# Channel attention and a gated convolution: v turned by VectorE instead of TensorE

## The chip, the cores and the metric

The kernel runs on one core of a Trainium2 chip. The metric is the device time in microseconds. Three runs of the kernel before took 652.89, 653.17 and 653.32 us; the median is 653.17 us.

Names used below: PE is TensorE, DVE is VectorE, ACT is ScalarE, POOL is GpSimd, and SP is SyncE, which here only issues transfers. A "step" is one chunk of the output's rows going through the second half of the kernel; a "group" is three rows per partition of q and k going through the first half.

## The reference

q, k and v have the shape 4 × 6336 × 256 (batch, row, channel), in float32.

```python
qn = q / (np.linalg.norm(q, axis=1, keepdims=True) + 1e-06)
kn = k / (np.linalg.norm(k, axis=1, keepdims=True) + 1e-06)
s = kn.transpose(0, 2, 1) @ qn / tau          # 256 x 256 for each batch
s = s - s.max(-1, keepdims=True)
a = np.exp(s)
a /= a.sum(-1, keepdims=True) + 1e-09
x = v @ a                                     # 6336 x 256 for each batch
gate_pre[t] = sum over 5 taps k of conv_w[k] * x[t - 4 + k]
gate = 1 / (1 + exp(-gate_pre))
out = (gate * (x @ w_val)) @ w_out
```

The attention is over channels: for each batch a matrix of 256 × 256 is made from all 6336 rows of q and k, and then all rows of v go through it.

## The kernel before

**Scores.** For each batch, partition p takes 49 rows of q and k, and 64 rows are left over. They go in 17 groups of up to three rows per partition (`score_group`). For a row, PE multiplies the 128 × 256 block of k (as weights, in two halves of 128 channels) with the block of q, and sums into a PSUM tile. A row is done in one of two ways. A native row multiplies the float32 data as they are (`nw` is the number of such rows in a group). A split row is first cut by ACT into a rounded high half in float32r (line 196) and by POOL into the remainder (line 197), and three products high·high, high·low and low·high follow. ACT squares q and k (line 213), and DVE and POOL add the squares up for the norms (line 218; `nv` rows of a group go to DVE). All of batch 0 is native but for the last row of its last two groups, and so are the first four groups of batch 1.

**Softmax.** `softmax` turns the sum into the attention matrix and a second matrix, attention times w_val, each as high and low halves. It is cut into stages that `tick` places between other work.

**Chunks.** The 6336 rows go in 13 chunks of up to 508 rows, 52 steps for the four batches. A chunk of v has four more rows ahead of it (the taps reach back). `load_v` brings it into SBUF with rows on partitions, in pieces of 1 KB. `transpose_v` turns it so that channels lie on partitions: PE transposes up to eight blocks of 128 × 128 into two PSUM tiles (line 359), ACT casts each into the high half (line 360), and DVE subtracts for the low half (line 361). `conv` multiplies with the attention matrix (six matmuls for each half of the output channels, line 369), and applies the taps: ACT the first (line 383), DVE the other four (line 385). `sigmoid` follows on ACT. `value` multiplies the same v with the second matrix (line 369 again) and DVE multiplies by the gate (line 398). `split_g` cuts the product into halves on ACT (line 411) and POOL (line 412). `finish` multiplies with w_out (line 428), ACT copies the result out of PSUM (line 438) and issues the stores.

**Order.** First come the 17 groups of batch 0; near their end the first chunks of v are loaded. Then the first four groups of batch 1 and the softmax of batch 0 are woven together. Then a loop over the 52 steps does for step n: load the chunk of v three steps on; one score group; the sigmoid of this step, the convolution of the next, the value and the split of this step; perhaps a second score group; the transposes of the chunk two steps on (`VLEAD` is 2); and `finish` of the step before. The score groups of all batches are spread over the first 36 steps, 47 groups in all, so the last steps have chunks alone. A planner, with its own model of times, places the instructions into each engine's queue; `behind` tells it to place work after a marked instruction, and `high_priority` raises a stage. Each engine works through its queue in order.

**Buffers.** The raw rows of q and k have six buffers, v's raw chunk three, the turned chunk three, the gate two. Four PSUM tiles are shared by the transposes, the values and the outputs; the convolution has two of its own. All loads are issued by SP in order, four groups ahead of use for q and k (`PREFETCH`).

Of the kernel before, what the change touches and what calls it, by code (L numbers as in the profile page):

```python
# [18 lines left out]
P = 128  # L19
# [3 lines left out]
VLEAD = 2  # L23
SIDE, LAST = 5, 15
# [5 lines left out]
def kernel(  # L30
# [76 lines left out]
    def load_weights(*names):  # L107
        for part in names:
            w = parts_w[part]
            if WORDS == 2:  # L110
                tag = {"val": "gate", "out": "o_sb"}.get(part)
                raw = (w_p if tag else const).tile([P, w.shape[1], WORDS], I32, name="w_raw", tag=tag or "c_raw")
            else:
                raw = w.rearrange("p (n o) -> p n o", o=1)
            w_raw[part] = raw
            if part == "conv":
                src = conv_w.bitcast(I32) if WORDS == 2 else conv_w
                nc.sync.dma_start(out=tau_sb, in_=tau.broadcast_to([P, 1]))
                for h in range(NH):
                    nc.sync.dma_start(out=raw[:, h * K:(h + 1) * K, :],  # L120
                                      in_=src[:, h * P * WORDS:(h + 1) * P * WORDS].rearrange("k (p o) -> p k o", o=WORDS))
            else:
                src = {"val": w_val, "out": w_out}[part]
                src = src.bitcast(I32) if WORDS == 2 else src
                nc.sync.dma_start(out=raw.rearrange("p (h e) o -> p h (e o)", h=NH),
                                  in_=src.rearrange("(h p) e -> p h e", p=P))
# [40 lines left out]

    state = {}

    def score_group(b, g):  # L170
# [4 lines left out]
        if b == 0:  # L175
            nw, nv = (2, 3) if g >= LAST else (GROUP, 2 if g < SIDE or g % 3 == 0 else 1)
        else:
            nw, nv = (GROUP, 1 if g else 2) if b == 1 and g < LEAD else (0, 2)
# [43 lines left out]
        def mms(np_, j):  # L222
            r = slice(0, np_)
            stop = g == NG - 1 and np_ == parts[-1][0] and j == parts[-1][1] + parts[-1][2] - 1
            for h in range(NH):
                hs = slice(h * P, (h + 1) * P)
                if j < nw:
                    ops = [(raw[r, j, 1, hs], raw[r, j, 0, :])]
                else:
                    ops = [(hi[r, j, 1, x, hs], hi[r, j, 0, y, :]) for x, y in ((0, 0), (0, 1), (1, 0))]  # L230
                for n_, (lhs, rhs) in enumerate(ops):
                    marks["PE"] = nc.tensor.matmul(st["s"][:, h, :], lhs, rhs, start=False,  # L232
                                                   stop=stop and h == NH - 1 and n_ == len(ops) - 1)
# [17 lines left out]
    def softmax(b):  # L251
# [9 lines left out]
        for x in range(2):  # L261
            for h in range(NH):
                marks["PE"] = nc.tensor.matmul(n_ps[:, x * NH + h:x * NH + h + 1], acc[:, x, h * P:(h + 1) * P], ones[:, 0:1],
                                               start=True, stop=True)
# [67 lines left out]
    vraw, vt = {}, {}  # L332

    def load_v(b, i):

        t0, w = chunks[i]
        t = raw_p.tile([P, NT, C], F32, name="v_raw", bufs=3)
        j0 = 0
        if i == 0:
            nc.gpsimd.memset(t[0:HALO, 0, :], 0.0)  # L340
            nc.sync.dma_start(out=t[HALO:P, 0, :], in_=v[b, 0:P - HALO])
            j0 = 1
        full, rest = divmod(HALO + w, P)
        lo = t0 - HALO
        nc.sync.dma_start(out=t[:, j0:full, :], in_=v[b, lo + j0 * P:lo + full * P].rearrange("(j p) c -> p j c", p=P))
        if rest:
            nc.sync.dma_start(out=t[0:rest, full, :], in_=v[b, lo + full * P:t0 + w])
        vraw[b, i] = t

    def transpose_v(b, i, h):  # L350
        w = HALO + chunks[i][1]
        if h == 0:
            vt[b, i] = [v_p.tile([P, NH, HALO + WMAX], F32R, name=name) for name in ("v_hi", "v_lo")]
        th, tl = vt[b, i]
        src = vraw[b, i]
        tp = ps.tile([P, 512], F32, name="t_ps", tag="bank")
        for j in range(-(-w // P)):
            np_ = min(P, w - j * P)
            marks["PE"] = nc.tensor.transpose(tp[:, j * P:j * P + np_], src[0:np_, j, h * P:(h + 1) * P], ident[0:np_, 0:np_])  # L359
        nc.scalar.copy(th[:, h, 0:w], tp[:, 0:w])  # L360
        nc.vector.tensor_tensor(tl[:, h, 0:w], tp[:, 0:w], th[:, h, 0:w].bitcast(F32), ALU.subtract)

    def product(ps, wt, which, b, i, h, lo, hi_):
        th, tl = vt[b, i]
# [11 lines left out]
    def conv(b, i, h):  # L376
        w = chunks[i][1]
        if h == 0:
            gates[b, i] = w_p.tile([P, NH, WMAX], F32, name="gate")
# [4 lines left out]
        for tap in range(1, K):  # L384
            nc.vector.scalar_tensor_tensor(gate[:, h, 0:w], x_ps[:, tap:tap + w], cw[:, h, tap:tap + 1],  # L385
                                           gate[:, h, 0:w], ALU.mult, ALU.add)

# [113 lines left out]
    for n in range(NG):  # L501
# [6 lines left out]
        if n == NG - 4:  # L508
# [4 lines left out]
            with tc.issue_after(last_load[0].ins):  # L513
                for nv in range(1, VLEAD + 1):
# [11 lines left out]
    with tc.high_priority(), behind("PE", "ACT"):  # L526
        for h in range(NH):
            transpose_v(*step(0), h)
# [22 lines left out]
    for h in range(NH):  # L551
        transpose_v(*step(1), h)
# [9 lines left out]
    for n in range(len(all_steps)):  # L562
        now, after, prev, new = step(n), step(n + 1), step(n - 1), step(n + VLEAD)
        if step(n + VLEAD + 1):
            load_v(*step(n + VLEAD + 1))
# [31 lines left out]
        if new:  # L597
            for h in range(NH):
                transpose_v(*new, h)
# [37 lines left out]
```

## Time and profile before

| | |
|---|---|
| median of three runs | 653.17 us |
| the profiled execution, its own time | 653.89 us |
| its span, first to last instruction | 651.9 us |
| PE busy | 637.9 us, 98% |
| DVE busy | 508.2 us, 78% |
| ACT busy | 466.6 us, 72% |
| POOL busy | 372.6 us, 57% |
| DMA | 105.77 MB, mean 162 GB/s |
| granted TensorE clock | 0.999 |

The time is what one launch takes on the device. The span lies between the first and the last instruction of the one execution that was profiled. Matmuls overlap each other in the records, so that PE's busy time isn't its useful time: what counts is how far apart their starts are. Where a row says "L361 DVE ... x96 | 62.8, 680 | 9.3", the group is line 361 on DVE, 96 instructions, 62.8 us busy together (overlaps counted once), 680 ns for a single one, and DVE was idle for 9.3 us just ahead of them.

### The profile page before, as it was taken

The page shows a single profiled execution, that of the slowest core. Times are in us where ns is not written, and L with a number is a line of the kernel's source. Part 1 is how long each engine was busy: PE and PEld are TensorE (multiplying, and loading weights), DVE is VectorE, ACT ScalarE, POOL GpSimd, SP SyncE. Part 2 cuts the span into 40 slices and gives each one's busy share as a digit, 9 for nine tenths or more (in the row PEclk, how much of TensorE's full clock was granted, in tenths as well). Part 3 has the DMA queues.
Part 4 walks back from the last instruction along what each step waited for, and adds up shares of the span by engine and source line. Part 5 has one row for each costly group of instructions (what it writes and reads, how often), then busy time and mean ns, then how long its engine had stood idle before and what let it go on. Part 6 is the DMA issues. An engine that isn't in the chain of part 4 may idle for free.

```text
span 651.9 us, 10735 instructions
## 1 busy us (share of the span) xinstructions
PE 637.9 (98%) x4040; PEld 572.4 (88%) x4040; DVE 508.2 (78%) x831; ACT 466.6 (72%) x612; POOL 372.6 (57%) x181
## 2 busy tenths in 40 slices
PE   8999899999999999999999999999999899999996
PEld 6888698999988998999988999999989798988886
DVE  3785798878858787777877788787777879888894
ACT  4566978768698886777679887686877765655564
POOL 1690887849654886767755489495763122212221
PEclk9999999999999999999999999999999999999999
DMA  8999564645544664545544466453222233343113
GB/s 275 378 336 365 181 209 151 210 139 170 172 127 152 211 191 143 184 148 159 184 144 162 137 203 213 151 169 96 90 68 85 97 123 111 105 130 109 62 50 101
DMA packets 75108, 105.77 MB, mean 162 GB/s; under 512 B 5744, under 2 KB 58160, under 8 KB 75056
## 3 DMA queue, kind: packets, MB, share of 16 engines
q1 hardware_dynamic: 49280, 79.76, 37.1%
q10 hardware_dynamic: 25776, 25.32, 12.4%
q8 instruction: 32, 0.52, 0.3%
q14 instruction: 20, 0.16, 0.1%
HBM read 79.11 MB, written 25.95 MB: 161 GB/s over the span
## 4 chain that ended last, share of the span: by engine, by line
PE 82%; DMA 6%; ACT 5%; POOL 3%; issue 1%; SPq 1%; ACTq 0%; DVE 0%; POOLq 0%
PE o_ps L428 21%; PE x_ps L369 20%; PE val_ps L369 19%; PE s_ps L232 15%; PE t_ps L359 6%; DMA raw<-in_k_dram 3%; POOL hi L197 2%; DMA w_raw<-in_moe_w_val_dram 2%; DMA raw<-in_q_dram 1%; ACT sq L213 1%; POOL acc L218 1%; PE o_ps L318 1%; ACT hi L196 1%; DMA w_raw<-in_moe_w_out_dram 1%; SPq L75 1%
## 5 line engine op out<-in xcount | busy, mean ns | idle before, releaser
L385 DVE SCALAR_TENSOR_TENSOR gate<-x_ps,wa,gate 128x508 f32<-128x508 f32 (+1 forms) x416 | 273.9, 716 | 15.8 <-ACT gate L383 14.7
L197 POOL TENSOR_TENSOR hi<-raw,hi 128x1536 fp32r<-128x1536 f32 (+2 forms) x51 | 166.0, 3257 | 103.3 <-ACT hi L196 103.3
L412 POOL TENSOR_TENSOR g_lo<-gate,g_hi 128x1016 fp32r<-128x1016 f32 (+1 forms) x50 | 117.5, 2351 | 125.8 <-ACT g_hi L411 125.8
L218 DVE TENSOR_TENSOR acc_ps<-acc_ps,sq 128x512 f32<-128x512 f32 (+1 forms) x124 | 86.5, 698 | 80.6 <-ACT sq L213 78.7
L369 PE MATMUL x_ps<-v_hi,w 128*128 128x512 f32 (+1 forms) x416 | 138.6, 392 | 0.5 <-DVE gate L385 0.3
L369 PE MATMUL val_ps<-v_hi,w 128*128 128x508 f32 (+1 forms) x416 | 134.1, 382 | 0.6 <-DVE w L323 0.5
L232 PE MATMUL s_ps<-hi 128*128 128x256 f32 (+1 forms) x846 | 119.6, 286 | 2.8 <-POOL hi L197 2.8
L232 PEld LDWEIGHTS s_ps<-hi 128*128 128x128 f32 (+1 forms) x846 | 109.6, 190 | 7.1 <-POOL hi L197 3.6
L428 PE MATMUL o_ps<-wo_hi,g_hi 128*128 128x256 f32 x400 | 112.9, 282 | 1.4 <-ACT at L313 1.4
L438 ACT COPY o_sb<-o_ps 128x512 f32<-128x512 f32 x99 | 58.2, 590 | 76.9 <-PE o_ps L428 76.7
L428 PE MATMUL o_ps<-wo_lo,g_hi 128*128 128x256 f32 x400 | 112.2, 281 | 0.0
L428 PE MATMUL o_ps<-wo_hi,g_lo 128*128 128x256 f32 x400 | 112.0, 280 | 0.0
L218 POOL TENSOR_TENSOR acc<-acc,sq 128x512 f32<-128x512 f32 x68 | 88.0, 1294 | 35.2 <-ACT sq L213 34.0
L213 ACT ACTIVATE sq<-raw 128x1536 f32<-128x1536 f32 (+3 forms) x69 | 95.8, 1393 | 16.4 <-POOL acc L218 8.7
L369 PEld LDWEIGHTS x_ps<-v_hi,w 128*128 128x128 f32 x416 | 77.4, 188 | 16.1 <-DVE gate L385 1.7
L369 PEld LDWEIGHTS val_ps<-v_hi,w 128*128 128x128 f32 x416 | 77.1, 188 | 14.4 <-DVE w L323 1.0
L383 ACT ACTIVATE gate<-x_ps,wa 128x508 f32<-128x508 f32 (+1 forms) x104 | 68.1, 669 | 18.8 <-PE x_ps L369 18.1
L398 DVE TENSOR_TENSOR gate<-val_ps,gate 128x508 f32<-128x508 f32 (+1 forms) x104 | 64.3, 657 | 21.7 <-ACT gate L391 20.0
L369 PE MATMUL x_ps<-v_lo,w 128*128 128x512 f32 (+1 forms) x208 | 79.6, 383 | 0.0
L369 PE MATMUL val_ps<-v_lo,w 128*128 128x508 f32 (+1 forms) x208 | 79.1, 380 | 0.0
L360 ACT CAST v_hi<-t_ps 128x512 fp32r<-128x512 f32 (+1 forms) x104 | 55.5, 570 | 32.9 <-PE t_ps L359 30.3
L428 PEld LDWEIGHTS o_ps<-wo_hi,g_hi 128*128 128x128 f32 x400 | 75.3, 188 | 2.4 <-ACT at L313 1.6
(80 smaller groups left out, 798.7 us busy)
## 6 DMA issues: line engine op xcount, KB each, us to landing
raw<-in_q_dram SPq DMA_DIRECT2D x64, 384.0 KB
raw<-in_k_dram SPq DMA_DIRECT2D x64, 384.0 KB
v_raw<-in_v_dram SPq DMA_DIRECT2D x44, 512.0 KB
out_dram<-o_sb ACTq DMA_DIRECT2D x47, 384.0 KB
out_dram<-o_sb ACTq DMA_DIRECT2D x47, 124.0 KB
v_raw<-in_v_dram SPq DMA_DIRECT2D x4, 384.0 KB
raw<-in_q_dram SPq DMA_DIRECT2D x4, 128.0 KB
raw<-in_k_dram SPq DMA_DIRECT2D x4, 128.0 KB
```

The lines of the kernel that those rows point to most:

```text
L197: nc.gpsimd.tensor_tensor(hi[r, js, :, 1, :], raw[r, js, :, :], hi[r, js, :, 0, :].bitcast(F32), ALU.subtract)
L213: nc.scalar.activation(sq[0:np_, ja:jb], raw[0:np_, ja:jb], AF.Square)
L218: add = eng.tensor_tensor(st[key][0:np_], st[key][0:np_], sq[0:np_, j], ALU.add)
L232: marks["PE"] = nc.tensor.matmul(st["s"][:, h, :], lhs, rhs, start=False, stop=stop and h == NH - 1 and n_ == len(ops) - 1)
L360: nc.scalar.copy(th[:, h, 0:w], tp[:, 0:w])
L369: marks["PRODUCT"] = nc.tensor.matmul(ps, wt[:, which, ws, ch, hs], vs[:, ch, lo:hi_], start=n_ == 0, stop=n_ == 3 * NH - 1)
L383: nc.scalar.activation(gate[:, h, 0:w], x_ps[:, 0:w], AF.Copy, scale=cw[:, h, 0:1])
L385: nc.vector.scalar_tensor_tensor(gate[:, h, 0:w], x_ps[:, tap:tap + w], cw[:, h, tap:tap + 1], gate[:, h, 0:w], ALU.mult, ALU.add)
L398: nc.vector.tensor_tensor(gate[:, h, 0:w], val_ps[:, 0:w], gate[:, h, 0:w], ALU.mult)
L412: nc.gpsimd.tensor_tensor(gl[:, :, 0:w], gate[:, :, 0:w], gh[:, :, 0:w].bitcast(F32), ALU.subtract)
L428: nc.tensor.matmul(o_ps[:, u * C:(u + 1) * C], gs[:, h, off:off + P], ws[:, h, :], start=n_ == 0, stop=n_ == 3 * NH - 1)
L438: marks["ACT"] = nc.scalar.copy(o_sb[:, j:j + len(pair), :], o_ps[:, 0:len(pair) * C].rearrange("p (j c) -> p j c", c=C))
```

## The change

The chunk of v is no longer turned by PE. `load_v` cuts it by channels into four quadrants: 64 channels, 256 bytes of each row, go to each group of 32 partitions, row r of each 32 rows on partition r of the group. So there are four transfers for a chunk where there was one (and four more for the first rows of a batch), and a chunk is rounded up to whole blocks of 32 rows. One DVE instruction then transposes all blocks of 32 × 32 in place. Its blocks take every second channel: on partition p lie channels 2p and 2p + 1 after it, as two halves. ACT casts both halves in one instruction, and POOL, no longer DVE, subtracts for the low halves.

Since the channels of v are now dealt out in this manner, the channels of k are too: `dealt` takes every second column of k as weights in the score matmuls and in the norms' sum.

Further edits: v is loaded four steps ahead instead of three, with four raw buffers; the gate has three buffers; in batches 1 to 3 the odd groups have one native row (unless all their rows are native already); and once all score groups are split, the last tap of the first half of the channels is done by ACT (a product into a spare tile) and POOL (the sum), except for the last step.

The core of the diff; `span_v` finds the rounded chunk's first row, its length and where the wanted rows start in it:

```diff
-            nw, nv = (GROUP, 1 if g else 2) if b == 1 and g < LEAD else (0, 2)
+            nw, nv = (GROUP, 1 if g else 2) if b == 1 and g < LEAD else (g % 2, 2)
...
+    def dealt(row, h):
+        return row.rearrange("p (c h) -> p h c", h=NH)[:, h]
...
-                    ops = [(raw[r, j, 1, hs], raw[r, j, 0, :])]
+                    ops = [(dealt(raw[r, j, 1, :], h), raw[r, j, 0, :])]
...
-                    ops = [(hi[r, j, 1, x, hs], hi[r, j, 0, y, :]) for x, y in ((0, 0), (0, 1), (1, 0))]
+                    ops = [(dealt(hi[r, j, 1, x, :], h), hi[r, j, 0, y, :]) for x, y in ((0, 0), (0, 1), (1, 0))]
...
+    def span_v(i):
+        t0, w = chunks[i]
+        cols = -(-(HALO + w) // Q) * Q
+        base = min(t0 - HALO, N - cols)
+        return base, cols, t0 - HALO - base
...
+        t = raw_p.tile([P, VW // Q, NH * Q], F32, name="v_raw", bufs=4)
+        for j in range(P // Q):
+            part = t[j * Q:(j + 1) * Q]
+            src = v[b, :, j * NH * Q:(j + 1) * NH * Q]
...
+            nc.sync.dma_start(out=part[:, g0:g, :],
+                              in_=src[base + g0 * Q:base + cols].rearrange("(g r) q -> r g q", r=Q))
...
-            marks["PE"] = nc.tensor.transpose(tp[:, j * P:j * P + np_], src[0:np_, j, h * P:(h + 1) * P], ident[0:np_, 0:np_])
-        nc.scalar.copy(th[:, h, 0:w], tp[:, 0:w])
-        nc.vector.tensor_tensor(tl[:, h, 0:w], tp[:, 0:w], th[:, h, 0:w].bitcast(F32), ALU.subtract)
+        t = vraw.pop((b, i))[:, 0:g, :].rearrange("p g (q h) -> p h g q", h=NH)
+        nc.vector.transpose(t, t)
+        marks["V"] = nc.scalar.copy(th[:, :, 0:g, :], t)
+        nc.gpsimd.tensor_tensor(tl[:, :, 0:g, :], t, th[:, :, 0:g, :].bitcast(F32), ALU.subtract)
...
-            gates[b, i] = w_p.tile([P, NH, WMAX], F32, name="gate")
+            gates[b, i] = w_p.tile([P, NH, WMAX], F32, name="gate", bufs=3)
...
-        for tap in range(1, K):
+        shared = h == 0 and issued == len(all_groups) and (b, i) != all_steps[-1]
+        for tap in range(1, K - shared):
...
+        if shared:
+            part = split_p.tile([P, WMAX], F32, name="part", tag="sq", bufs=2)[:, 0:w]
+            nc.scalar.activation(part, x_ps[:, K - 1:K - 1 + w], AF.Copy, scale=cw[:, h, K - 1:K])
+            nc.gpsimd.tensor_tensor(gate[:, h, 0:w], gate[:, h, 0:w], part, ALU.add)
...
-                for nv in range(1, VLEAD + 1):
+                for nv in range(1, VLEAD + 2):
...
-        if step(n + VLEAD + 1):
-            load_v(*step(n + VLEAD + 1))
+        if step(n + VLEAD + 2):
+            load_v(*step(n + VLEAD + 2))
```

More of the change, by code (lines that the diff above doesn't have):

```diff
@@ L23 @@
 VLEAD = 2
+Q = 32
 SIDE, LAST = 5, 15
@@ L111, in load_weights @@
                 tag = {"val": "gate", "out": "o_sb"}.get(part)
-                raw = (w_p if tag else const).tile([P, w.shape[1], WORDS], I32, name="w_raw", tag=tag or "c_raw")
+                raw = (w_p if tag else const).tile([P, w.shape[1], WORDS], I32, name="w_raw", tag=tag or "c_raw", bufs={"val": 3, "out": 2}.get(part, 1))
             else:
@@ L262, in softmax @@
             for h in range(NH):
-                marks["PE"] = nc.tensor.matmul(n_ps[:, x * NH + h:x * NH + h + 1], acc[:, x, h * P:(h + 1) * P], ones[:, 0:1],
-                                               start=True, stop=True)
+                lhs = dealt(acc[:, x, :], h) if x else acc[:, x, h * P:(h + 1) * P]
+                marks["PE"] = nc.tensor.matmul(n_ps[:, x * NH + h:x * NH + h + 1], lhs, ones[:, 0:1], start=True, stop=True)
         yield
@@ L332 @@
     vraw, vt = {}, {}
-    def load_v(b, i):
[L336 to L347, printed above, removed]
-        vraw[b, i] = t
@@ L350, in transpose_v @@
[L350 to L361, printed above, removed]
+    VW = -(-(HALO + WMAX) // Q) * Q
@@ new lines, in span_v @@
+    def span_v(i):
[3 more added lines that the diff above has]
+        return base, cols, t0 - HALO - base
+    def load_v(b, i):
+        base, cols, _ = span_v(i)
+        g = cols // Q
+        t = raw_p.tile([P, VW // Q, NH * Q], F32, name="v_raw", bufs=4)
+        for j in range(P // Q):
+            part = t[j * Q:(j + 1) * Q]
+            src = v[b, :, j * NH * Q:(j + 1) * NH * Q]
+            g0 = 0
+            if base < 0:
+                nc.gpsimd.memset(part[0:-base, 0, :], 0.0)
+                nc.sync.dma_start(out=part[-base:Q, 0, :], in_=src[0:Q + base])
+                g0 = 1
+            nc.sync.dma_start(out=part[:, g0:g, :],
+                              in_=src[base + g0 * Q:base + cols].rearrange("(g r) q -> r g q", r=Q))
+        vraw[b, i] = t
@@ L363, in product, with transpose_v @@
+    def transpose_v(b, i):
+        g = span_v(i)[1] // Q
+        th, tl = vt[b, i] = [v_p.tile([P, NH, VW // Q, Q], F32R, name=name) for name in ("v_hi", "v_lo")]
+        t = vraw.pop((b, i))[:, 0:g, :].rearrange("p g (q h) -> p h g q", h=NH)
+        nc.vector.transpose(t, t)
+        marks["V"] = nc.scalar.copy(th[:, :, 0:g, :], t)
+        nc.gpsimd.tensor_tensor(tl[:, :, 0:g, :], t, th[:, :, 0:g, :].bitcast(F32), ALU.subtract)
     def product(ps, wt, which, b, i, h, lo, hi_):
-        th, tl = vt[b, i]
+        th, tl = (t.rearrange("p h g q -> p h (g q)") for t in vt[b, i])
+        at = span_v(i)[2]
+        lo, hi_ = at + lo, at + hi_
@@ L525 @@
     tick()
-    with tc.high_priority(), behind("PE", "ACT"):
-        for h in range(NH):
-            transpose_v(*step(0), h)
+    with tc.high_priority(), behind("ACT"):
+        transpose_v(*step(0))
     with behind("PE", "ACT"):
@@ L550 @@
             nc.scalar.copy(wo_hi.rearrange("p h e -> p (h e)"), w_raw["out"][:, :, 1].bitcast(F32))
-    for h in range(NH):
-        transpose_v(*step(1), h)
+    for n in range(1, VLEAD):
+        transpose_v(*step(n))
     with behind("ACT"):
@@ L597 @@
         if new:
-            for h in range(NH):
-                transpose_v(*new, h)
+            transpose_v(*new)
         tick()
```

1 line of the change is left out of this document (removed).

## The prediction

> **What bounds the kernel now.** I read the page's busy times and its chain first, then the stretches, then the waits of PE and POOL. A change off PE can only pay where PE is not the bound.
>
> ```profile
> span 651.9 us, 10735 instructions
> PE 637.9 (98%) x4040; PEld 572.4 (88%) x4040; DVE 508.2 (78%) x831; ACT 466.6 (72%) x612; POOL 372.6 (57%) x181
> ...
> q1 hardware_dynamic: 49280, 79.76, 37.1%
> q10 hardware_dynamic: 25776, 25.32, 12.4%
> ...
> PE 82%; DMA 6%; ACT 5%; POOL 3%; issue 1%; SPq 1%; ACTq 0%; DVE 0%; POOLq 0%
> PE o_ps L428 21%; PE x_ps L369 20%; PE val_ps L369 19%; PE s_ps L232 15%; PE t_ps L359 6%; DMA raw<-in_k_dram 3%; POOL hi L197 2%; DMA w_raw<-in_moe_w_val_dram 2%; DMA raw<-in_q_dram 1%; ACT sq L213 1%; POOL acc L218 1%; PE o_ps L318 1%; ACT hi L196 1%; DMA w_raw<-in_moe_w_out_dram 1%; SPq L75 1%
> ```
>
> The stretches: the first row is the main part (score groups beside chunks), the second the tail (chunks alone), the third three steps of the main part, with four score groups in them. Columns: length, then busy time and instructions of PE, weight loads, DVE, ACT, POOL.
>
> ```profile
> 78.00:501.00 423.00, 421.76 (x2796) 384.05 (x2795) 336.67 (x543) 328.80 (x416) 293.61 (x128) 1.00 0.49 157
> 501.00:640.00 139.00, 137.24 (x855) 121.64 (x854) 118.28 (x191) 84.73 (x134) 36.37 (x16) 1.00 0.31 98
> 420.00:456.00 36.00, 36.00 (x241) 32.90 (x240) 28.48 (x45) 26.76 (x33) 26.27 (x11) 1.00 0.41 132
> ```
>
> What PE, and then POOL, waited for in the main part:
>
> ```profile
> PE s_ps L232 <- POOL hi L197: 1.2, 2, 0.6
> ...
> POOL hi L197 <- ACT hi L196: 102.3, 33, 6.0
> POOL g_lo L412 <- ACT g_hi L411: 18.1, 20, 2.9
> ```
>
> PE is full from 78 to 640 us and waits for others 1.2 us in the main part. Work taken off PE therefore shortens the time, as long as another engine does not reach the new pace. POOL is 73% busy in the three steps; its idle time is spent waiting for ACT's casts.
>
> **PE loses the transposes.** Eight of them, timed from start to the start of the next instruction, and their group over the kernel:
>
> ```profile
> 437.92 1.03 PE L359 MATMUL t_ps<-ident,v_raw 128*128 128x128 f32 x8
> ...
> 438.70 0.37 PE L232 MATMUL s_ps<-hi 128*128 128x256 f32 x1
> ```
> ```profile
> L359 PE MATMUL t_ps<-ident,v_raw x400: 262/272/328, 50.7 to 627.7; 128*128 128x128 f32 x131, 116*128 116x116 f32 x3
> ```
>
> 8 take 0.78 us there, 98 ns each, so 400 take 39 us. The chain's 6% of 651.9 is the same 39 us: all of it lies on the path. **−39.2 us.**
>
> **PE gains the native rows.** In batches 1 to 3 every odd group (outside the four groups already native) multiplies one row in float32: 6 + 8 + 8 = 22 rows. The native and the split pace:
>
> ```profile
> 29.65 18.08 PE L232 MATMUL s_ps<-raw 128*128 128x256 f32 x83
> ```
> ```profile
> 87.17 2.15 PE s_ps L232 x18
> ```
>
> A native row is two matmuls of two instructions each (118 native matmuls of before stand as 236 records), 4 × 0.218 = 0.87 us; a split row is 6 × 0.119 = 0.72 us. 22 × 0.15 = **+3.4 us**. In return ACT and POOL handle 1024 instead of 1536 elements there.
>
> **POOL takes the low halves of v.** Its rows:
>
> ```profile
> L197 POOL TENSOR_TENSOR hi<-raw,hi 128x1536 fp32r<-128x1536 f32 x45 | 158.4, 3520 | 93.3 <-ACT hi L196 93.3
> L412 POOL TENSOR_TENSOR g_lo<-gate,g_hi 128x1016 fp32r<-128x1016 f32 x47 | 113.8, 2421 | 121.6 <-ACT g_hi L411 121.5
> L361 DVE TENSOR_TENSOR v_lo<-t_ps,v_hi 128x512 fp32r<-128x512 f32 x96 | 62.8, 680 | 9.3 <-ACT v_hi L360 9.3
> L411 ACT CAST g_hi<-gate 128x1016 fp32r<-128x1016 f32 x47 | 49.2, 1046 | 2.1 <-DVE gate L398 2.0
> L360 ACT CAST v_hi<-t_ps 128x512 fp32r<-128x512 f32 x96 | 52.8, 587 | 30.6 <-PE t_ps L359 28.0 <-DMA out_dram<-o_sb 2.6
> L361 DVE TENSOR_TENSOR v_lo<-t_ps,v_hi 128x244 fp32r<-128x244 f32 x8 | 3.1, 401 | 0.4 <-ACT v_hi L360 0.4
> ```
>
> The v subtraction of a whole chunk is the form of L412: 2.42 us. Three steps: 26.27 + 3 × 2.42 − 1.87 × 1.10 (22 of 47 groups, 3.52 − 2.42 each) = 31.5 us. PE's three steps become 36.0 − 24 × 0.098 + 1.87 × 0.15 = 33.9 us. POOL goes from 73% to 93%: it still fits, barely. POOL serves in order, so a split that PE needs can stand behind a v or gate subtraction of 2.4 us; today PE waits hardly at all. Bounds of the stall this makes: nothing if the order absorbs it, and 4.3 us in three steps if half of POOL's present 9.7 us of idle time cannot be filled. I take 0.35 us in three steps, **+4 us** over the twelve such periods (423 / 36) of the main part, because the subtraction of v is due only a step after it is issued and so can fill gaps. POOL, ACT and DVE also read v with a step of two words, which no row shows: no cost at the one end, a second pass at the other (2.42 us more on POOL, 38.8 us in three steps, a pace of 13). I take none, as for the weights below.
>
> **DVE turns v.** No row shows its transpose. DVE costs 401 ns for 244 elements and 680 for 512, 1.04 ns an element, so 1024 elements estimate to 1.21 us. Below stands half of that, above twice (each word moved in two passes); I take 1.21 as the nearest row's rate. It replaces two subtractions of 62.8 / 96 = 0.65 us busy: three steps come to 28.48 − 3.9 + 3.6 = 28.2 of 33.9 us. At twice the price they come to 31.8, still below PE. **Nothing on the path.** ACT casts 1024 elements once (1.05 us, L411) instead of 512 twice (52.8 / 96 = 0.55 us busy each): nothing.
>
> **The tail.** PE's step of 9.16 us (matmul starts below) shrinks by 0.78 us to 8.4:
>
> ```profile
> 557.71 2.82 PE o_ps L428 x24
> ...
> 566.87 2.83 PE o_ps L428 x24
> ```
>
> ```profile
> L385 DVE SCALAR_TENSOR_TENSOR gate<-x_ps,wa,gate 128x508 f32<-128x508 f32 x384 | 261.0, 737 | 15.2 <-ACT gate L383 14.1
> L218 POOL TENSOR_TENSOR acc<-acc,sq 128x512 f32<-128x512 f32 x68 | 88.0, 1294 | 35.2 <-ACT sq L213 34.0
> L383 ACT ACTIVATE gate<-x_ps,wa 128x508 f32<-128x508 f32 x96 | 64.8, 687 | 18.7 <-PE x_ps L369 18.1
> ```
>
> There one of eight taps (261.0 / 384 = 0.68 us busy) leaves DVE for ACT (0.69) and POOL (1.29, by its 512-element add). DVE: 118.28 × 9.16 / 139 = 7.8 us a step, less 1.30 and 0.68, plus 1.21, is 7.0; ACT 5.6 + 0.7; POOL 2.4 + 2.4 + 1.3 = 6.1. All lie under 8.4. The POOL add runs while DVE does the second half's four taps (2.7 us). If that cover were gone, the sigmoid would wait up to 1.3 us a step. The third gate buffer and the wider tiles cost no time.
>
> **DMA.** The two queue rows give 12.4% × 16 × 651.9 / 25776 = 50.2 ns for 982 bytes and 78.5 ns for 1618 bytes: 6.5 ns a packet plus 0.0445 ns a byte. A 256-byte packet estimates to 17.9 ns, a chunk (2048 over 16 engines) to 2.3 us against 1.6 us. Bounds: 11.4 ns (bytes only) and 50.2 ns (no cheaper than the present packet). At 17.9 three steps need 3 × 2.3 + 4 × 2.3 + 3 × 1.6 = 21 of 33.9 us. SP issues four transfers instead of one, about 0.4 us each, 1.2 us more a step; SP's own waits on v (below) are 300.7 / 44 = 6.8 us each, so it has the time. These waits now end with ACT's cast and POOL's subtraction of a chunk instead of PE's transposes; raw loads stand behind them on SP and the score groups wait for those, four groups ahead, about three steps.
>
> The Trainium skill, "DMA: Bandwidth & Descriptors", section Specifications, says that line rate wants 512 bytes or more a transfer. By a flat 50.2 ns the three steps would need 33 of 33.9 us, and only the opening would pay.
>
> ```profile
> SPq L345 <- PE t_ps L359: 300.7, 44, 14.7
> ```
>
> In the opening, three v chunks instead of two stand ahead of the loads for batch 1's group 3: 6.9 us of DMA against 3.2, **+3.7 us of delay**. PE uses that group in the second half of these matmuls, from 60.6 us; its first load landed at 56.4, the other was issued 1.4 us after it:
>
> ```profile
> 57.94 5.35 PE L232 MATMUL s_ps<-raw 128*128 128x256 f32 x24
> ```
> ```profile
> 47.08 9.28 DMA raw<-in_q_dram
> ```
> ```profile
> 48.52 0.74 SPq L75 DMA_DIRECT2D raw<-in_k_dram  x1
> ```
>
> So slack is near 2.7 us, and I take **+1.5 us**; bounds nothing and 13 us (at 50.2 ns: 19.2 − 3.2 − 2.7).
>
> **The strided weight loads.** Score matmuls load every second column of k. No row shows a strided load. The bounds are no cost, and a second pass. Their contiguous row lies at the matmul's pace, so I take nothing and leave the other end to a rival.
>
> **Sum.** The profiled execution took 653.89 us, span 651.9 and 2.0 around it; the median 653.17 is 0.7 lower. 653.9 − 39.2 + 3.4 + 4 + 1.5 = 623.6, as a median **623 us**.
>
> **The rivals.** *POOL paces the main part.* For it: 93% and strict order; against: its waits are on ACT, which runs earlier relative to it once it lags. With half of the 9.7 us kept idle, three steps take 31.5 + 4.3 = 35.8 us; the main part gains 12 × 0.2 = 2 us, opening and tail keep 16 × 0.78 = 12 us, and 1.5 is lost: 641 us.
>
> *The transpose keeps POOL out.* While DVE transposes, POOL's access stands still: 31.5 + 3 × 1.21 = 35.1 us in three steps. The main part gains 12 × 0.9 = 11, the tail 12, the opening loses 1.5: 632 us. In the main part before, DVE always has an operand in PSUM, so no row speaks.
> The Trainium skill, "SBUF — State Buffer", section Who interferes with whom, states such a lock between VectorE in two-port modes and GpSimd; no run here shows whether a transpose is one.
>
> *The weight loads pay for the stride.* This ends slower.
>
> ```profile
> L232 PEld LDWEIGHTS s_ps<-hi 128*128 128x128 f32 x834 | 108.0, 190 | 6.6 <-POOL hi L197 3.6
> ```
>
> After the change (141 − 22) × 6 = 714 split matmuls remain. A load takes at most the 98 ns of a transpose, which loads 128 columns too; doubled it is 196 against the matmul's 119 ns: +77 ns × 714 = 55 us, giving 678 us. Native rows (218 ns) hide it. It decides from 30 / 714 = 42 ns extra a load on. Against it: 190 ns is the latency, not the pace, and the row gives no sign of a bandwidth limit.
>
> **How the numbers follow.** Forecast 0.53 (613 to 632 by itself), POOL paces (by its waits) 0.20, transpose locks POOL 0.14, weight loads 0.10, everything cancels 0.03. The range 612 to 643 leaves out the weight loads, the cancelling case and the outer edge of the rest. Faster than 0.2% (the least a measurement of this kernel can tell from no change): 0.87; same 0.02; slower 0.11.
>
> **What would show it.** Right: no t_ps on PE, a main-part row with PE full and POOL above 90%, DVE's transpose near 1.2 us, s_ps<-hi still 0.119 us apart, a tail step of 8.4 us. Wrong: PE waits on POOL's hi above 15 us in all (POOL paces), POOL's subtractions longer than 2.42 and 3.52 us (lock), x18 score groups above 2.15 us (stride), a raw load awaited around 60 us (DMA).

## The result, and the profile after

The changed kernel took **625.59 us**, the median of four runs (624.62 to 627.29); the kernel before, on the same chip, 653.07 us (652.89 to 653.32). The ratio is 0.9582, with an interval of 0.9559 to 0.9605: 27.5 us less, 4.2%. The forecast was 623 us in a range of 612 to 643. The profiled execution took 626.16 us. In the experiments below, one execution of the kernel with 11 native rows took 999 us at a granted clock of 0.556, and its figures leave that one out.

The head of the page after:

```profile
span 624.4 us, 10237 instructions
PE 601.3 (96%) x3596; PEld 537.6 (86%) x3596; DVE 499.1 (80%) x763; ACT 470.8 (75%) x576; POOL 489.7 (78%) x261
```

PE has lost 37 us of busy time and POOL has gained 117. DVE has hardly changed, since a transpose took the place of two subtractions. Of the four engines PE is still the fullest.

The main part, and three of its steps with four score groups, by stretches of the kernel after. Columns: stretch, length, then busy time and instructions of PE, weight loads, DVE, ACT, POOL, then granted clock, DMA share and GB/s.

```profile
78.00:475.00 397.00, 396.54 (x2494) 359.60 (x2493) 335.52 (x509) 323.52 (x382) 355.34 (x174) 1.00 0.62 173
381.52:413.10 31.58, 31.58 (x200) 28.67 (x199) 28.96 (x43) 26.20 (x30) 30.97 (x15) 1.00 0.65 191
```

And what PE waited for in that main part:

```profile
PE x_ps L378 <- DVE gate L395: 0.3, 1, 0.3
```

PE is full. Beside it POOL is busy for 355.34 of 397.00 us, 90%, and in the three steps for 30.97 of 31.58 us, 98%. There both engines are near their limit, and PE hardly waits for POOL.

Where the time went is read from the stores: ACT issues the first store of a step when the step's output is there. Here are those of steps 0, 34, 48 and 49 in the kernel before, and then in the kernel after (start, duration, queue, line):

```profile
98.01 0.43 ACTq L443 DMA_DIRECT2D out_dram<-o_sb  x1
...
505.42 0.39 ACTq L443 DMA_DIRECT2D out_dram<-o_sb  x1
...
634.18 0.38 ACTq L443 DMA_DIRECT2D out_dram<-o_sb  x1
641.08 0.38 ACTq L443 DMA_DIRECT2D out_dram<-o_sb  x1
```
```profile
101.79 0.42 ACTq L457 DMA_DIRECT2D out_dram<-o_sb  x1
...
480.87 0.38 ACTq L457 DMA_DIRECT2D out_dram<-o_sb  x1
...
601.92 0.38 ACTq L457 DMA_DIRECT2D out_dram<-o_sb  x1
613.66 0.38 ACTq L457 DMA_DIRECT2D out_dram<-o_sb  x1
```

The removed transposes of PE can be dealt to the same stretches. These rows of the kernel before show them alone (the first number behind the length is PE's):

```profile
0.00:98.01 98.01, 4.47 (x32) 3.79 (x32) 5.28 (x8) 4.45 (x8) 1.00 0.83 290
98.01:505.42 407.41, 36.53 (x264) 31.10 (x264) 42.60 (x67) 36.45 (x68) 1.00 0.48 154
505.42:651.90 146.48, 13.76 (x104) 12.12 (x104) 18.05 (x29) 14.59 (x28) 1.00 0.31 99
```

With 98 ns (the prediction's price) for each of 32, 264 and 104 transposes, and the prediction's other terms put where it put them, its sum stands beside the measured one so:

| stretch | forecast | measured | difference |
|---|---|---|---|
| to the first store of step 0 | −3.1 + 1.5 = −1.6 | +3.8 | +5.4 |
| from there to that of step 34 | −25.9 + 3.4 + 4 = −18.5 | −28.3 | −9.8 |
| from there to the end | −10.2 | −3.0 | +7.2 |
| sum | −30.3 | −27.5 | +2.8 |

The total was 2.8 us off, but the three stretches were 5 to 10 us off each. The measured column comes from one trace of each kernel. The experiments look for these three errors, and ask whether POOL was near to being the bound.

### The profile page after: what moved, and what is told of

The parts are those of the page before. It is cut to its first block, busy times and chain, and to the rows that moved or that the text cites. A ratio compares the mean times of both kernels' runs of the same rounds, so it can differ in the third digit from the quotient of the medians.

```text
span 624.4 us, 10237 instructions
## 1 busy us (share of the span) xinstructions
PE 601.3 (96%) x3596; PEld 537.6 (86%) x3596; DVE 499.1 (80%) x763; ACT 470.8 (75%) x576; POOL 489.7 (78%) x261
## 4 chain that ended last, share of the span: by engine, by line
PE 70%; DMA 9%; POOL 5%; ACT 5%; DVE 4%; SPq 4%; issue 3%; ACTq 0%; POOLq 0%; DVEq 0%
PE s_ps L235 18%; PE o_ps L442 17%; PE x_ps L378 17%; PE val_ps L378 16%; DMA v_raw<-in_v_dram 5%; SPq L358 3%; POOL v_lo L368 2%; DVE gate L395 2%; DMA raw<-in_q_dram 2%; DMA raw<-in_k_dram 1%; POOL hi L201 1%; PE o_ps L321 1%; DVE v_raw L366 1%; DMA out_dram<-o_sb 1%; ACT hi L200 1%
## 5 line engine op out<-in xcount | busy, mean ns | idle before, releaser
L201 POOL TENSOR_TENSOR hi<-raw,hi 128x1536 fp32r<-128x1536 f32 (+3 forms) x51 | 142.2, 2789 | 20.8 <-ACT hi L200 17.3
L368 POOL TENSOR_TENSOR v_lo<-v_raw,v_hi 128x1024 fp32r<-128x1024 f32 (+1 forms) x52 | 123.2, 2370 | 35.4 <-ACT v_hi L367 29.7
L378 PE MATMUL x_ps<-v_hi,w 128*128 128x512 f32 (+1 forms) x416 | 141.6, 389 | 6.2 <-DVE gate L395 3.5
L378 PE MATMUL val_ps<-v_hi,w 128*128 128x508 f32 (+1 forms) x416 | 135.8, 386 | 3.0 <-DVE w L326 2.2
L222 DVE TENSOR_TENSOR acc_ps<-acc_ps,sq 128x512 f32<-128x512 f32 (+1 forms) x124 | 85.7, 691 | 29.4 <-ACT sq L217 25.9
L442 PE MATMUL o_ps<-wo_hi,g_lo 128*128 128x256 f32 x400 | 108.2, 283 | 0.0
L217 ACT ACTIVATE sq<-raw 128x1536 f32<-128x1536 f32 (+3 forms) x69 | 95.9, 1394 | 14.9 <-DMA raw<-in_k_dram 7.9
L366 DVE STREAM_TRANSPOSE v_raw<-v_raw 128x1024 f32<-128x1024 f32 (+1 forms) x52 | 62.5, 1203 | 45.5 <-DMA v_raw<-in_v_dram 32.9
L235 PE MATMUL s_ps<-hi 128*128 128x256 f32 (+1 forms) x714 | 97.2, 286 | 0.0
L392 ACT ACTIVATE gate<-x_ps,wa 128x508 f32<-128x508 f32 (+1 forms) x104 | 68.3, 664 | 35.8 <-PE x_ps L378 35.5
L235 PEld LDWEIGHTS s_ps<-hi 128*128 128x128 f32 (+1 forms) x714 | 91.7, 195 | 2.1
```

Of the source, the lines that this page charges most:

```text
L201: nc.gpsimd.tensor_tensor(hi[r, js, :, 1, :], raw[r, js, :, :], hi[r, js, :, 0, :].bitcast(F32), ALU.subtract)
L217: nc.scalar.activation(sq[0:np_, ja:jb], raw[0:np_, ja:jb], AF.Square)
L222: add = eng.tensor_tensor(st[key][0:np_], st[key][0:np_], sq[0:np_, j], ALU.add)
L366: nc.vector.transpose(t, t)
L368: nc.gpsimd.tensor_tensor(tl[:, :, 0:g, :], t, th[:, :, 0:g, :].bitcast(F32), ALU.subtract)
L378: marks["PRODUCT"] = nc.tensor.matmul(ps, wt[:, which, ws, ch, hs], vs[:, ch, lo:hi_], start=n_ == 0, stop=n_ == 3 * NH - 1)
```

## The experiments

### The native rows: none, half, one in every group

```diff
-(g % 2, 2)
+(0, 2)                    # e5_no_native
+(g % 4 == 1, 2)           # e10_native_half
+(1 if g else 0, 2)        # e11_native_all
```

> The changed kernel with all rows of batches 1 to 3 split as before (no native row in odd groups). Theory A, POOL has room in the main part: PE gains 3.4 us and the time is 621 to 624 us. Theory B, the native rows keep POOL below its limit: three steps on POOL rise from 31.5 to 33.5 of PE's 33.6 us, PE waits on the splits again, 627 to 634 us.

> Half of the native rows: one in every fourth group of batches 1 to 3 (3 + 4 + 4 = 11 rows instead of 22). Without any the time was 650.3 us, with 22 it was 625.6. Theory A (POOL sets the pace as soon as it is full, and every native row takes 1.1 us of its queue): the loss is steady with the number of rows, 633 to 643 us, and POOL stands above 91% over the main part. Theory B (the rows matter by their place, because every odd group needs one for the order of POOL's queue to hold): the time lies at 645 us or above. Theory C (a few rows are enough to fill the gap between PE's and POOL's paces): 624 to 630 us.

> One native row in every group of batches 1 to 3 but the first of a batch (13 + 16 + 16 = 45 rows instead of 22). PE gains 23 x 0.15 = 3.4 us of work, POOL loses 23 x 1.1 = 25 us. Theory A (with 22 rows PE is the bound of the main part and POOL no longer stops it): 627 to 631 us, POOL near 84% of the main part, and the step of the main part longer by 0.1 us. Theory B (POOL still costs the main part something with 22 rows): 618 to 625 us.

| native rows in batches 1 to 3 beyond those of before | time (lowest to highest), us | ratio to before |
|---|---|---|
| 0 | 650.34 (648.18 to 653.52) | 0.9965 [0.9946, 0.9985] |
| 11 | 637.98 (637.53 to 639.14) | 0.9774 [0.9757, 0.9790] |
| 22 (the change) | 625.59 (624.62 to 627.29) | 0.9582 [0.9559, 0.9605] |
| 45 | 634.58 (632.87 to 638.23) | 0.9724 [0.9685, 0.9764] |

Without the native rows nearly the whole gain is gone, more than either theory had given, though PE has less to do. A native row spares POOL 512 elements, 1.10 us. So 22 rows are worth 24.2 us of POOL's queue, and the time rose by 24.8; 11 rows are worth 12.1, and it rose by 12.4. These are the sizes that a main part paced by POOL would give, but the traces don't show one. Here is the stretch from the first store to that of step 34, first without native rows, then in the kernel after (columns as above), and then two of PE's waits without native rows (total, times, longest):

```profile
105.49:500.98 395.49, 380.01 (x2421) 343.06 (x2420) 319.30 (x487) 312.83 (x366) 355.67 (x166) 0.99 0.57 158
```
```profile
101.79:480.87 379.08, 378.74 (x2392) 343.81 (x2391) 320.23 (x488) 311.51 (x371) 336.10 (x165) 1.00 0.59 166
```
```profile
PE o_ps L312 <- ACT a L302: 10.2, 3, 5.7
...
PE s_ps L235 <- POOL hi L201: 3.9, 3, 1.6
```

POOL is busy for 90% of the first stretch and 89% of the second. The first is 16.4 us longer, and PE is short of work for 15.5 us of it; in the second PE is full. PE's two longest waits, 4.1 and 5.7 us, are for the softmax at the end of a batch's scores and not for POOL's splits. They lie between the stores of steps 21 and 22, and of steps 34 and 36. There this kernel takes 8.0 and 6.3 us more than the kernel after, over half of the 27.2 us between the two profiled executions. The granted clock has a part too: its mean is 0.979 here and 0.993 after, which I estimate at some 9 us of PE's time at most (2.1% of 651.4 us against 0.7% of 624.4). So it is shown that the 22 native rows are worth some 25 us; that POOL's pace is the whole reason is not.

The case of 11 rows lies in the range of its first theory, but its trace doesn't show the steady loss of that theory. The lead over the kernel before is the same as the changed kernel's up to the store of step 21 (15.3 us against 14.9), and between steps 21 and 22 this kernel takes 20.0 us against 11.0. This is that place, in order of time, from the timelines of five queues (start, duration, engine, line; in brackets what the engine had waited for):

```profile
334.55 2.41 POOL L201 TENSOR_TENSOR hi<-raw,hi 128x1024 fp32r<-128x1024 f32 x1 [4.96 <-ACT hi L200]
...
335.85 0.66 ACT L367 CAST v_hi<-v_raw 128x512 fp32r<-128x512 f32 x1
...
336.92 1.32 POOL L368 TENSOR_TENSOR v_lo<-v_raw,v_hi 128x512 fp32r<-128x512 f32 x1
...
338.26 1.92 SPq L358 DMA_DIRECT2D v_raw<-in_v_dram  x4
...
346.85 1.25 DVE L366 STREAM_TRANSPOSE v_raw<-v_raw 128x1024 f32<-128x1024 f32 x1 [4.44 <-DMA raw<-in_q_dram]
...
348.78 0.80 PE L378 MATMUL x_ps<-v_hi,w 128*128 128x512 f32 x1 [4.83 <-DVE gate L395]
```

POOL's subtraction frees a raw buffer of v at 338.24, SP issues the load into it 0.02 us later, and DVE's queue stands at a transpose for 4.44 us until a load is in. (The row names a load of q. The transpose reads v alone, so the load that it wants must be one of v that landed with it; this is inferred.) The four taps behind the transpose are late, and PE waits for them 4.83 us. A late subtraction thus becomes a late load, and a late load stops DVE and then PE. But POOL wasn't full there: it had just waited 4.96 us for a cast of ACT, and the cast of the chunk itself came only at 335.85. Behind PE's wait the clock is halved up to 354.36 (last section), some 2.8 us more (half of the 5.58 us from 348.78 on). So most of these 9 us, and of the 12.4 us with them, are one stop of this kind and not POOL's pace.

With 45 rows POOL is relieved (464.0 us busy instead of 489.7), and the time is 9.0 us longer than with 22, where PE's extra work explains 3.4. The waits of PE and DVE in that kernel, and DVE's in the kernel after (total, times, longest):

```profile
PE x_ps L378 <- DVE gate L395: 11.3, 9, 2.2
...
DVE v_raw L366 <- DMA v_raw<-in_v_dram: 42.1, 27, 5.0
```
```profile
DVE v_raw L366 <- DMA v_raw<-in_v_dram: 32.9, 25, 3.0
```

PE waits 11.3 us for the taps, against 3.5 us in the kernel after, and DVE stands 9.2 us longer at its transposes. The longer waits fit a cost in DVE's order instead of POOL's load; that the standing transposes cause them in full isn't shown. The forecasts, which rested on PE and POOL alone, both missed.

### PE's transposes put back beside DVE's

```diff
+        for h in range(NH):
+            tp = ps.tile([P, 512], F32, name="t_ps", tag="bank")
+            for j in range(g // NH // 2):
+                nc.tensor.transpose(tp[:, j * P:(j + 1) * P], ident, ident)
         nc.vector.transpose(t, t)
```

> The changed kernel with the eight transposes of a chunk put back on PE, reading a constant and read by nothing. Theory A, PE is the bound all along and each transpose costs its 98 ns: 625.6 + 36 to 40, 661 to 666 us. Theory B, other engines pace the changed kernel, in the tail above all, and part of the transposes hides in PE's waits: 645 to 658 us.

Measured: 657.71 us (654.90 to 659.39), ratio 1.0072 [1.0048, 1.0095]. That is 32.1 us more than the changed kernel. By the store of step 34 the kernel is already 31.6 us behind it, and from there to the store of step 49 only 0.6 us more are lost, though about 100 of the 400 transposes lie there. So PE's work sets the pace of the main part, and in the tail it doesn't: there 10 us of PE work go in at hardly any cost, while PE's idle time between these stores falls from 8.2 to 1.2 us. The time lies in the range of the second theory, which had named the tail.

### The last tap not shared

```diff
-        shared = h == 0 and issued == len(all_groups) and (b, i) != all_steps[-1]
+        shared = False
```

> The changed kernel (625.6 us) with the last tap of the first half back on DVE in the tail. Theory A, the shared tap holds the convolution's PSUM tile until ACT reaches it in its queue and so delays PE: the tail's waits of PE on ACT's part (2.7 us) go, 621 to 625 us. Theory B, the tap takes needed work off DVE: DVE rises by 0.68 us to 7.7 of 8.4 us a step, 626 to 632 us.

Measured: 631.41 us (630.84 to 633.84), ratio 0.9677 [0.9657, 0.9698]: 5.8 us slower than the change, so that the sharing does help, as the second theory said. Up to 467 us its instructions are those of the change, in the same order, and yet its first store comes 1.8 us earlier and that of step 34 3.0 us earlier. So far apart are two executions of the same instructions, and smaller differences between two traces say nothing. From step 34 to step 49 it takes 140.7 us, against 132.8 in the change and 135.7 in the kernel before. Its waits of PE in the tail:

```profile
PE o_ps L442 <- POOL g_lo L426: 6.8, 5, 1.8
PE x_ps L378 <- DVE gate L395: 4.2, 4, 1.9
```

In the tail PE thus waits for the chain through DVE's taps, ACT and POOL's last subtraction. Without the sharing there is no gain there at all. The prediction had put the sharing down as hidden, and gave the tail to PE.

### How v is loaded: whole rows, five buffers, fewer chunks early

The first edit brings each row of v in one piece of 1 KB onto a partition, as the kernel before does, and leaves the rest of the change as it is. DVE's blocks then hold other elements of v, so the output's rows and channels are in other places:

```diff
-        for j in range(P // Q):
-            part = t[j * Q:(j + 1) * Q]
-            src = v[b, :, j * NH * Q:(j + 1) * NH * Q]
...
+        rows = t.rearrange("p g q -> p (g q)").rearrange("p (j c) -> p j c", c=C)
...
+        nc.sync.dma_start(out=rows[:, j0:cols // P, :],
+                          in_=v[b, base + j0 * P:base + cols].rearrange("(j p) c -> p j c", p=P))
```

> The changed kernel with v loaded as before, one transfer in pieces of 1 KB, into a tile of the same size; the transpose and all that follows run on the same sizes, but channels and rows lie elsewhere, so the output isn't the reference's. Theory A, the 256-byte pieces cost the opening about 4 us (first store 3.8 us later than before) and let loads come late in the tail: 617 to 622 us, and the first store at 98 us or earlier. Theory B, the opening is late because of DVE and ACT order, not of the transfers: 624 to 627 us.

Measured: 627.18 us (625.86 to 629.80), ratio 0.9610 [0.9584, 0.9636]. The first store of step 0 comes at 95.92 us instead of 101.79, and instead of 99.97 in the run above, whose opening is the same as the change's. So the small pieces, with the four transfers in place of one, cost **4 to 6 us in the opening**, as the first theory said; its time was missed. At step 34 the lead over the change is still 5.7 us (2.7 over the run above). Then it is all lost again: from step 34 to step 49 this kernel is 2.2 us slower than the kernel before. An earlier start is of no use here, as the tail takes longer. Why it takes longer isn't settled; PE's longest wait there is again for the last subtraction on POOL (6.2 us in four waits).

```diff
-        t = raw_p.tile([P, VW // Q, NH * Q], F32, name="v_raw", bufs=4)
+        t = raw_p.tile([P, VW // Q, NH * Q], F32, name="v_raw", bufs=5)
```

> The changed kernel with five raw buffers for v instead of four, loads issued at the same place. Theory A, the long steps of the tail come from loads of v that wait on SP until POOL has subtracted the chunk in the buffer: with one buffer more the wait moves a step back, SP's waits on POOL's subtraction fall below 80 us from 194, 617 to 622 us. Theory B, the long steps come from the order on DVE and ACT: 624 to 628 us.

Measured: 628.48 us (626.37 to 630.33), ratio 0.9634 [0.9612, 0.9657]. A fifth buffer doesn't help, although DVE waits 32.9 us for loads of v in the kernel after. SP's waits for POOL's subtraction stay at 185.8 us, far above the 80 of the first theory, and DVE's for loads of v at 40.5.

```diff
-                for nv in range(1, VLEAD + 2):
+                for nv in range(1, VLEAD):
                     load_v(*step(nv))
...
-        if step(n + VLEAD + 2):
-            load_v(*step(n + VLEAD + 2))
+        for nv in range(VLEAD if n == 0 else n + VLEAD + 2, n + VLEAD + 3):
+            if step(nv):
+                load_v(*step(nv))
```

> The changed kernel with only chunks 0 and 1 loaded in the opening, and chunks 2, 3 and 4 at the start of the loop. Theory A, the 256-byte loads ahead of batch 1's first groups make the opening late: two chunks of 3.6 us less stand ahead of them, the first store comes at 97 to 99 us instead of 101.8, and the time is 621 to 624 us. Theory B, the delay is only moved, because chunks 2 to 4 then stand ahead of the next groups: 625 to 628 us.

Measured: 624.54 us (623.70 to 626.37), ratio 0.9568 [0.9550, 0.9586]. The first store comes 2.1 us earlier than in the change, little more than the 1.8 us between two executions of the same instructions, and the end 1.1 us earlier; the intervals overlap, so that it can't be told from the change. With one native row in every group besides:

> One native row in every group but the first of a batch, and the chunks of v loaded as in the run with two chunks in the opening (624.5 us). Theory A (PE is the bound, the two edits add up): 1 us less than the run with one native row in every group, 626 to 630 us. Theory B (POOL is the bound, and the earlier start is kept): 617 to 623 us.

Measured: 633.77 us (630.12 to 634.70), ratio 0.9695 [0.9666, 0.9724], 0.8 us less than with 45 rows alone. The intervals overlap, so that this is no measured difference; both theories gave a lower time.

### The low half of v on DVE

```diff
-        nc.gpsimd.tensor_tensor(tl[:, :, 0:g, :], t, th[:, :, 0:g, :].bitcast(F32), ALU.subtract)
+        nc.vector.tensor_tensor(tl[:, :, 0:g, :], t, th[:, :, 0:g, :].bitcast(F32), ALU.subtract)
```

> The changed kernel with the subtraction of v given to DVE, on the same tiles, instead of POOL. Theory A, DVE has the less room: it rises to about 32 of 33.6 us in three steps and to 8.2 of 8.4 us in a step of the tail, so the main part slips by 0 to 10 us and the tail by more, 630 to 645 us. Theory B, POOL's long queue is what holds the changed kernel, and DVE absorbs the work: 618 to 625 us.

Measured: 705.29 us (704.43 to 710.21), ratio 1.0816 [1.0778, 1.0855], far beyond what was expected. Rows of its timeline, POOL and DVE together:

```profile
439.89 1.70 DVE L368 TENSOR_TENSOR v_lo<-v_raw,v_hi 128x1024 fp32r<-128x1024 f32 x1
440.47 3.39 POOL L201 TENSOR_TENSOR hi<-raw,hi 128x1024 fp32r<-128x1024 f32 x1
...
445.08 2.41 POOL L426 TENSOR_TENSOR g_lo<-gate,g_hi 128x1016 fp32r<-128x1016 f32 x1
445.33 3.24 DVE L368 TENSOR_TENSOR v_lo<-v_raw,v_hi 128x1024 fp32r<-128x1024 f32 x1
```

The POOL subtraction that begins during DVE's takes 3.39 us, against 2.42 in the kernel after. When POOL is first, DVE's takes 3.24 us; with no instruction of POOL beside it it takes 1.21 (at 52.60 for instance), and the 1.70 above has its own wait in it, behind a sum that POOL runs from 439.21 to 440.51. In both rows DVE's ends 1.08 us after POOL's: the one that starts later stands until the other is through. The Trainium skill, "SBUF — State Buffer", section Who interferes with whom, says that a VectorE instruction with two inputs in SBUF contends with a GpSimd instruction that reads SBUF; the rows agree. So with v no longer in PSUM, it was better that the subtraction left DVE too. The whole 80 us don't follow from this. DVE's busy time rises by 79 us, to 578.4 of 702.6, and so DVE still isn't full. PE waits 23.1 us for the last subtraction on POOL and 10.1 for its cast on ACT, and the mean granted clock falls to 0.962. How the rest divides isn't settled.

### The transposes held back

```diff
-        nc.vector.tensor_tensor(gate[:, h, 0:w], val_ps[:, 0:w], gate[:, h, 0:w], ALU.mult)
+        marks["VAL"] = nc.vector.tensor_tensor(gate[:, h, 0:w], val_ps[:, 0:w], gate[:, h, 0:w], ALU.mult)
...
         if new:
-            transpose_v(*new)
+            with behind("VAL"):
+                transpose_v(*new)
```

> The changed kernel with each transpose of the loop placed behind the step's last multiplication of value and gate on DVE. In the changed kernel the planner puts the transposes two to three chunks ahead of their casts, and there DVE's queue stands until the chunk's load has landed (32.9 us in all). Theory A, this standing delays the taps behind it and with them PE in the tail: DVE's waits on loads of v fall below 8 us, steps 38 to 41 run at 8.4 to 9 us, 617 to 622 us. Theory B, the tail is long because of the chain of taps, sigmoid, product and casts itself: 624 to 630 us.

The block holds back the chunk's cast and subtraction with its transpose.

Measured: 700.74 us (697.79 to 703.35), ratio 1.0721 [1.0680, 1.0763]; both theories missed it. DVE's wait for loads of v fell from 32.9 to 4.0 us, as was meant. But now the low halves come late:

```profile
PE o_ps L442 <- POOL g_lo L426: 28.0, 28, 2.0
PE s_ps L235 <- POOL hi L201: 16.1, 14, 2.9
```

So the waits of DVE at its transposes in the kernel after go with a lead that is worth more than they cost; what they cost there isn't shown. The mean granted clock is 0.973 here, against 0.993. How the 75 us come about in full isn't settled, since the order on ACT and POOL moved too.

## Why the prediction was right

**PE loses the transposes: right, but priced too low.** No t_ps stands on PE any more, the main part is full on PE, and adding 400 such transposes back cost 32.1 us of the 39.2, nearly all of it in the main part. The 98 ns came from the start of the next instruction, at 438.70. But that one, a single score matmul, takes longer than usual; the one behind it starts here:

```profile
438.91 0.39 PE L369 MATMUL x_ps<-v_hi,w 128*128 128x512 f32 x1
```

From 437.92 to 438.91 are 0.99 us; less 0.12 for the one score matmul, 0.87 us are left for eight transposes, 109 ns each. So 400 are worth 43.6 us instead of 39.2.

**The native rows: the price on PE right, their worth missed.** In the chain of waits of the kernel after, a group of three split rows, and then the two parts of a group with a native row:

```profile
143.05 2.15 PE s_ps L235 x18
...
147.48 0.86 PE s_ps L235 x4
...
152.29 1.44 PE s_ps L235 x12
```

0.86 + 1.44 = 2.30 us against 2.15: 0.15 us a row, as forecast. The prediction wrote "in return ACT and POOL handle 1024 instead of 1536 elements there", and put it into POOL's sum, but it didn't price the change without them. That kernel takes 650 us.

**POOL's stall: mis-sized, +4 against none.** The row of the main part has 0.3 us of waits. The step that failed is the choice of 0.35 us in three steps out of 0 to 4.3: the lower bound held. (The upper bound was off too: half of 9.7 is 4.85, and a POOL of 35.8 us would hold up PE's 33.9 by 1.9, not by 4.3.) The idle time that POOL had spent waiting for ACT was filled for the greater part: 98% in the three steps, where 93% had been worked out, 90% over the main part. Besides, the main part gained some 6 us that no term of the sum has (−28.3, where transposes and native rows give −22.5). At 109 ns the 264 transposes there are worth 28.8 us instead of 25.9, half of these 6. The other half isn't settled.

**POOL's and DVE's durations: right.** The groups of the kernel after, by shape (count, busy us, mean ns, idle before):

```profile
L368 POOL TENSOR_TENSOR v_lo<-v_raw,v_hi 128x1024 fp32r<-128x1024 f32 x48 | 118.0, 2458 | 28.1 <-ACT v_hi L367 22.6 <-DMA raw<-in_k_dram 5.5
...
L201 POOL TENSOR_TENSOR hi<-raw,hi 128x1536 fp32r<-128x1536 f32 x23 | 81.3, 3535 | 11.8 <-ACT hi L200 11.4 <-POOL g_lo L426 0.4
L201 POOL TENSOR_TENSOR hi<-raw,hi 128x1024 fp32r<-128x1024 f32 x22 | 53.2, 2419 | 4.6 <-DMA raw<-in_q_dram 2.9 <-ACT hi L200 1.5
```
```profile
L366 DVE STREAM_TRANSPOSE v_raw<-v_raw 128x1024 f32<-128x1024 f32 x48 | 59.7, 1244 | 43.2 <-DMA v_raw<-in_v_dram 32.2 <-POOL hi L201 5.3 <-DMA raw<-in_q_dram 2.4
```

The subtraction of v takes 2.46 us (2.42 forecast), the transpose 1.24 (1.21). Reading v with a step of two words costs POOL nothing that these rows show. POOL's other subtractions are as long as before (3.54 against 3.52 us), so the transpose doesn't keep POOL out: that rival fell. In the trace 24 of the 48 subtractions of v run beside a transpose, and they take 2.46 us like the others.

**The strided weight loads: right, nothing.** Eighteen score matmuls still take 2.15 us. The rival that ended slower fell with that row.

**The opening: mis-sized, +1.5 against 5 to 7.** The first store comes 3.8 us later than before (2.0 in the run without the shared tap), and 3.1 us should have been gained. SP's queue after, three chunks of v, and PE's waits behind it:

```profile
47.15 10.85 SPq L358 DMA_DIRECT2D v_raw<-in_v_dram  x12
```
```profile
64.10 2.84 PE L235 MATMUL s_ps<-raw 128*128 128x256 f32 x12 [1.66 <-DMA raw<-in_k_dram]
...
76.42 1.22 PE L378 MATMUL val_ps<-v_hi,w 128*128 128x508 f32 x2 [2.25 <-DVE w L326]
```

Issuing three chunks took 10.85 us, 3.6 us each, where 2.3 had been estimated from 17.9 ns a packet: 2048 packets over 16 engines in 3.6 us are 28 ns a packet. The packets' own records agree, 28.3 ns from 46 to 59 us, but give 18.4 ns from 102 to 470 us: the price was right for the main part and failed in the opening. That the raw load of k would be awaited was named (1.66 us, at 64 instead of 60 us). Not named was the second wait: the weights `w` of the first softmax stood on DVE behind a transpose that waited for its chunk of v. That is a wait which the change adds in front of everything on DVE, and the prediction looked for what stands behind it on SP only. Behind that wait the granted clock is 0.50 from 75.90 to 79.31 (last section); the kernel before and the run without the shared tap have no such stretch there.

**The tail: mis-sized, −10.2 against −3.0.** From step 36 to step 48 the kernel after takes 100.1 us for twelve steps against 107.2 before, 0.59 us less a step where 0.78 had been forecast. But this is not PE's pace, as the run with the added transposes shows: PE is idle 6.4 us of these 125:

```profile
475.00:600.00 125.00, 118.64 (x692) 103.15 (x691) 99.97 (x145) 87.69 (x123) 81.69 (x42) 1.00 0.37 97
```

No engine is full there. The step that failed is that PE stays the bound of the tail: the chain of taps, ACT and POOL from one step to the next takes over, as PE's waits in the run without the shared tap show. The sums of busy time under 8.4 us, from which the prediction concluded that PE stays the bound, say nothing on such a chain. And between the last two steps' stores 11.74 us pass instead of 6.90, of which the last section shows more.

The likeliest case was the right one, since the work left the engine that was the bound. That the total fell only 2.6 us above the forecast of 623 is luck: errors that add up to 22 us over the three stretches had two signs.

## What to carry to other kernels

When work is moved off the bound, sum up the new load of every engine that takes it over in the fullest stretch, and then look for what in the same change unloads it: here two edits on the side, the native rows and the shared tap, are worth 25 and 6 of the 27.5 us gained. Two engines may both be near 100% for some steps without a stall, but here both fewer and more native rows were slower. An instruction that waits for a load stops all that is queued behind it on its engine, so ask of each moved instruction what it now stands in front of.

## What the runs showed of the hardware beyond that

**A pause of PE under 2 us can halve its clock for the next 3.4 us.** PE near the end of the kernel after: one wait of 1.80 us, and then matmuls that start 0.21 us apart instead of 0.12; below, PE's busy time (behind the length) and the granted clock (the third number from the right) around there and around the wait in the opening.

```profile
607.73 0.35 PE L378 MATMUL x_ps<-v_hi,w 128*128 128x244 f32 x1 [1.80 <-DVE gate L395]
...
608.77 0.41 PE L442 MATMUL o_ps<-wo_lo,g_hi 128*128 128x256 f32 x1
608.98 0.41 PE L442 MATMUL o_ps<-wo_hi,g_lo 128*128 128x256 f32 x1
...
612.02 0.28 PE L442 MATMUL o_ps<-wo_hi,g_lo 128*128 128x256 f32 x1
612.14 0.28 PE L442 MATMUL o_ps<-wo_hi,g_hi 128*128 128x256 f32 x1
```
```profile
72.48:75.90 3.42, 1.63 (x6) 1.05 (x6) 2.66 (x4) 3.42 (x5) 2.26 (x2) 1.00 1.20 252
75.90:79.31 3.41, 2.89 (x7) 2.34 (x8) 3.03 (x5) 3.41 (x3) 3.41 (x3) 0.50 1.16 179
604.97:608.38 3.41, 1.61 (x14) 1.41 (x13) 2.85 (x6) 1.17 (x2) 1.62 (x2) 1.00 0.08 28
608.38:611.79 3.41, 3.41 (x19) 3.41 (x18) 3.27 (x8) 1.86 (x4) 1.29 (x1) 0.50 0.00 0
```

Some 15 matmuls lose 0.09 us each, 1.4 us beside the 1.80 of the wait: two thirds of the 4.8 us that the last step lost. With 11 native rows the wait of 4.83 us at 348.78 was followed by a clock of 0.50 until about 354. Not every pause does it: 2.20 us of waiting with 45 native rows (at 256.17) left the clock at 1.00. The low stretches last 3.41 us or twice that, and within a run they start a whole number of 3.41 us apart (608.38 − 75.90 is 156 times 3.413). So what counts here is a fixed row of such stretches. In the one ahead of a low clock PE was idle for 1.79 us (the first row) and 1.80 us (the third). The pause of 2.20 us fell into two of them:

```profile
252.23:255.64 3.41, 1.74 (x13) 1.45 (x11) 1.41 (x2) 0.00 (x0) 2.44 (x2) 1.00 0.11 28
255.64:259.05 3.41, 2.88 (x15) 2.55 (x16) 3.38 (x6) 2.44 (x4) 0.00 (x0) 1.00 0.72 154
```

PE was idle for 1.67 us in the first and 0.53 in the second. Over all the runs the border isn't sharp: every low clock behind the opening follows at least 1.70 us of idle time, and some stretches with 1.70 to 1.90 us weren't followed by one. The Trainium skill, "TensorE: Matmul & The Clock Gate", section HAM oscillation — how this bites in real kernels, warns of pauses above some 3.4 us; here 1.80 was enough. That the low clock lasts 3.41 us and keeps to a fixed row agrees with the free-running window of about 3.4 us in its section What's actually happening.

**Small pieces cost where the load is waited for, and only there.** The opening lost 4 to 6 us to pieces of 256 bytes, at 28.3 ns a packet. In the main part, from step 0 to step 34, the kernel with whole rows gained 28.2 us on the kernel before and the changed one 28.3, though its packets of v are four times as many, at 18.4 ns each.
